# Loading the first entry's v from another queue, uncast, beside q and k

## The chip, the cores and the metric

The kernel runs on one core of a Trainium2 chip. The metric is the device time of one execution in microseconds (us); lower is better. A profile of one execution stands beside the times; its clock starts at the span's start.

## The reference

The inputs are `q`, `k`, `v` of shape (8, 8, 576, 64): 8 entries, 8 heads, 576 positions, 64 channels, fp32. Per entry and head, with `gamma = 1 - 2^(-5-head)`:

```python
scores = scale * np.matmul(q, k.transpose(0, 1, 3, 2))
Dmat = np.where(rel >= 0, gamma[:, None, None] ** rel[None, :, :], 0.0)   # rel = i - j
attn = np.matmul(scores * Dmat, v)
x = attn.transpose(0, 2, 1, 3).reshape(4608, 512)
h = x @ w_in                                   # 512 x 2048
out = (h * (1.0 / (1.0 + np.exp(-1.702 * h)))) @ w_out   # 2048 x 512
```

So it is a retention layer (linear attention with a decay, no softmax) followed by a two-layer network on 4608 tokens.

## The kernel before, in words

**Retention.** Each entry's 576 positions are cut into five pieces of 128, 128, 128, 128 and 64 rows; piece `c` of entry `b` is step `n = 5b + c`, 40 steps in all. The decay is factored: v is multiplied by `vfac` (`gamma^-pos` times the scale) when it lies on chip (`scale_v`), and the result by `gq` (`gamma^pos`) when it is evacuated (`evac_o`). A step is: `transposes(n)` (TensorE turns q and k into `psT`), `evac_t` (ScalarE copies them to `qk`), `scores` into `psS`, `mask_s` (VectorE, `psS` to `sm`), and `values`: the masked scores times v into `psO`, then k times v added to the running state in `psZ`, then the state of the earlier pieces (`zs`, which `evac_z` copies from `psZ` on ScalarE) times q. `intra(n)` is `scores` and `mask_s`; `turn(n)` is `transposes`, `evac_t`, `scale_v`. `psS`, `psT`, `psZ` are single buffers, so the next step's writer waits for this step's reader.

**Network.** The tokens go in nine chunks of 512. `hidden(c, f)` makes one of 16 column blocks of the hidden layer (four matmuls, then the activation on ScalarE); `project(c, r, g)` makes a quarter (`g`) of the sum for 128 output rows (four matmuls), and after `g = 3` VectorE copies the bank to `osb` and SP stores it. Chunk 0 needs steps 0 to 3; chunk 1 needs steps 4 to 8.

**Order.** Everything is written out by hand in one program order; a small recorder (`Rec`) gives each engine its instructions in that order and adds semaphore waits from the tiles that are read and written. An engine never overtakes its own order. First the attention steps 0 to 3, with `fill(count)`: matmuls on a zero tile into `psH[0]` that nobody reads, between the steps. Then `hidden(0, 0..15)` with step 4 between them, then `project(0, ...)`, 16 of them, with the steps 5 to 8 between them after the indices that the dictionary `between` names (`burst(n)` is `intra(n)`, `values(n-1)`, `transposes(n+1)`, `evac_t`, `finish(n-1)`, `scale_v(n+1)`, where `finish` is `evac_o` and `evac_z`). Later chunks interleave `hidden`, `project` and bursts.

**Loads.** All loads are issued by Pool (GpSimd) and cast fp32 to bf16 on the way: `load(b, c)` one piece each of q, k and v (128 rows, 128 KB as bf16), `load_w_in(i)` and `load_w_out(i)` a quarter of each weight (512 KB as bf16). Each issue keeps Pool busy while it writes the transfer's descriptors. Pool also scales v of steps 1 to 3 (`scale_v(n, "POOL")`); VectorE scales step 0 and all from step 4 on. SP issues only the stores of the result and, from step 13 on, transposing transfers. Pool's order at the start, before:

```python
load(0,0,"qk"); load(0,1,"qk"); load(0,0,"v"); load(0,2,"qk"); load(0,1,"v")
load(0,3,"qk"); load(0,2,"v"); load(0,3,"v"); load_w_in(0); scale_v(1,"POOL")
load_w_in(1); scale_v(2,"POOL"); scale_v(3,"POOL"); load(0,4)
load_w_in(2..3); load_w_out(0..3)        # then load(1, c), load(2, c)
```

Of the kernel before, what the change touches and what calls it, by code (L numbers as in the profile page):

```python
# [7 lines left out]
ALU = mybir.AluOpType  # L8
BF16 = mybir.dt.bfloat16
FP32 = mybir.dt.float32  # L10

B = 8
H = 8
S = 576
DH = 64
# [107 lines left out]
def bass_retnet_parallel__then__act_gelu_quick_kernel(  # L123
# [8 lines left out]
    P = nc.NUM_PARTITIONS  # L132
    R = Rec()
    es = ExitStack()
    with es:
        def sb(name, shape, dtype):
            return es.enter_context(nc.sbuf_tensor(name, shape, dtype))
# [14 lines left out]
        vfac = sb("vfac", [P, H, NC], FP32)  # L152
        gq = sb("gq", [P, NC, HP, 128], FP32)
        st_q = sb("st_q", [P, NST, NC, H * DH], BF16)
        st_k = sb("st_k", [P, NST, NC, H * DH], BF16)
        st_v = sb("st_v", [P, NST, NC, H * DH], BF16)
        qk = [sb(f"qk{i}", [P, 2, HP, 128], BF16) for i in range(NQK)]
        sm = [sb(f"sm{i}", [P, 2, HP, 128], BF16) for i in range(3)]
        zs = [sb(f"zs{i}", [P, HP, 128], BF16) for i in range(2)]
# [17 lines left out]
        def load(b, c, what="qkv"):  # L177
            sl, rows = b % NST, ROWS[c]
            for nm, src, dst in (("q", q, st_q), ("k", k, st_k), ("v", v, st_v)):
                if nm not in what:  # L180
                    continue
                s = src[b, :, 128 * c : 128 * c + rows, :].rearrange("h p d -> p h d")
                d = dst[0:rows, sl, c, :].rearrange("p (h d) -> p h d", d=DH)
                R.op("POOL", lambda e, d=d, s=s: e.dma_start(d, s),  # L184
                     w=[(nm, sl, c)], dma=(nm, sl, c))

        def load_w_in(i):
            s = moe_w_in.rearrange("(a p) n -> p a n", p=128)[:, :, 512 * i : 512 * i + 512]
            R.op("POOL", lambda e: e.dma_start(w_in_sb[:, :, 512 * i : 512 * i + 512], s),
                 w=[("w_in", i)], dma=("w_in", i))  # L190
# [43 lines left out]
        def constants_third(a, b):  # L234
            for t, nm in ((st_q, "q"), (st_k, "k"), (st_v, "v")):
                R.op("DVE", lambda e, t=t: e.memset(t[64:128, a:b, 4, :], 0.0),
                     w=[(nm, sl, 4) for sl in range(a, b)])

        def later_gq(hp):
            R.op("ACT", lambda e: e.activation(  # L240
                gq[:, 1:NC, hp, :], posi.ap(), AF.Exp, scale=lng[:, hp : hp + 1]),
                r=["posi", ("lng", hp, 0), ("lng", hp, 1)], w=[("gq", 1)])
# [6 lines left out]
        def scale_v(n, eng="DVE"):  # L249
            b, c = divmod(n, NC)  # L250
            sl = b % NST
            t = st_v[:, sl, c, :].rearrange("p (h d) -> p h d", d=DH)
            f = vfac[:, :, c : c + 1].to_broadcast([P, H, DH])
            R.op(eng, lambda e: e.tensor_tensor(t, t, f, ALU.mult),  # L254
                 r=["vfac"], w=[("v", sl, c)])

        def transposes(n):
            b, c = divmod(n, NC)
            sl = b % NST

            def fn(e):
                for a, t in ((0, st_q), (1, st_k)):
                    for hp in range(HP):
                        i = e.matmul(psT[:, a, hp, :], t[:, sl, c, 128 * hp : 128 * hp + 128],  # L264
                                     ident.ap(), is_transpose=True)
                return i
            R.op("PE", fn, r=["ident", ("q", sl, c), ("k", sl, c)], ps=["T"])

        def evac_t(n):
            R.op("ACT", lambda e: e.activation(qk[n % NQK].ap(), psT.ap(), AF.Copy),  # L270
                 w=[("qk", n % NQK, 0), ("qk", n % NQK, 1)], ps=["T"])
# [85 lines left out]
        def dma_turn(n):  # L357
            b, c = divmod(n, NC)
            sl, N = b % NST, ROWS[c]
            for a, t, nm, rows in ((0, st_q, "q", N), (1, st_k, "k", P)):  # L360
                R.op("SP", lambda e, a=a, t=t, rows=rows: e.dma_start_transpose(
                    out=qk[n % NQK][:, a, :, 0:rows], in_=t[0:rows, sl, c, :]),
                    r=[(nm, sl, c)], w=[("qk", n % NQK, a)], dma=("turn", n % NQK, a))

        def turn(n):
            transposes(n)
            evac_t(n)
            scale_v(n)

        def intra(n):  # L370
            scores(n)
            mask_s(n)

        def finish(n):
            evac_o(n)
            if n % NC < 4:
                evac_z(n)
            b = n // NC + NST
            if n % NC == 4 and b < B:
                for c in range(NC):  # L380
                    load(b, c)

        def burst(n):
            if n < NSTEP:
                intra(n)
            values(n - 1)
            if n + 1 < PE_TURNS:
                transposes(n + 1)
                evac_t(n + 1)
            if PE_TURNS <= n + 3 < NSTEP:  # L390
                dma_turn(n + 3)
            finish(n - 1)
            if n + 1 < NSTEP:
                scale_v(n + 1)
# [38 lines left out]

        constants_first()
        load(0, 0, "qk")
        load(0, 1, "qk")
        load(0, 0, "v")
        load(0, 2, "qk")
        load(0, 1, "v")
        load(0, 3, "qk")  # L440
        load(0, 2, "v")
        load(0, 3, "v")
        load_w_in(0)
        scale_v(1, "POOL")
        load_w_in(1)
        scale_v(2, "POOL")
        scale_v(3, "POOL")
        constants_third(0, 1)
        load(0, 4)
        for i in range(2, 4):  # L450
            load_w_in(i)
        for i in range(4):
            load_w_out(i)

        def fill(count):
            def fn(e):
                for _ in range(count):
                    i = e.matmul(psH[0].ap(), idle[:, 0:128], idle.ap(), start=True, stop=True)  # L458
                return i
            R.op("PE", fn, r=["idle"], ps=[("H", 0)])  # L460
# [13 lines left out]
        transposes(1)  # L474
        evac_t(1)
        later_gq(2)
        fill(4)
        intra(1)
        transposes(2)
        evac_t(2)  # L480
        scale_v(0)
        fill(4)
        intra(2)
        values(0, third[0])
        evac_z(0)
# [31 lines left out]
        between = {1: lambda: turn(4), 4: lambda: intra(4), 8: finish_4}  # L517
# [13 lines left out]
        def intra_9():  # L531
            intra(9)
            turn(10)

        between = {4: lambda: turn(5), 6: burst_5, 8: lambda: burst(6), 10: lambda: burst(7),
                   12: lambda: burst(8), 14: values_8}
        for i in range(16):
            r, g = divmod(i, 4)
            project(0, r, g, *wide[r % 3])
            if i in between:  # L540
                between[i]()
        between = {0: intra_9, 3: lambda: burst(10), 6: lambda: burst(11),
                   9: lambda: burst(12), 12: lambda: burst(13)}
# [93 lines left out]
```

## Time and profile before

| | |
|---|---|
| median of 3 runs | 317.63 us (317.32 to 317.97) |
| profiled execution, its own time | 317.39 us |
| its span in the trace | 315.6 us |
| TensorE busy | 304.1 us (96%), granted clock 1.00 |
| VectorE, ScalarE, Pool busy | 119.9, 130.8, 110.5 us |
| DMA engines | busy 9 tenths or more up to about 166 us |
| Pool's transfers | 116736 packets, 18.36 MB as written |

The busy share of TensorE is an average over the whole span. What it leaves idle lies in the first 41 us, at the very end, and in small pieces between. A transfer's time to landing runs from the start of its issue to the point where its semaphore shows it complete.

### The profile page before, as it was taken

The numbers are of one execution on the slowest core, as the hardware profiler recorded it, in microseconds if no ns is written. First come the engines' busy times: TensorE is split into PE (matmuls) and PEld (weight loads), VectorE is DVE, ScalarE is ACT, GpSimd is POOL, SyncE is SP. The second block draws the span as 40 slices with busy tenths as digits, with TensorE's granted clock in tenths as the row PEclk, the third lists the DMA queues.
The fourth block names the chain that finished last, engine by engine and source line by source line (L and its number), as shares of the span: only waits on it lengthen the run. The fifth ranks groups of instructions, "written<-read, shape, count | busy, mean of one in ns | idle before, by whom it ended". The sixth has DMA issues, their size and how long they took to land.

```text
span 315.6 us, 5372 instructions
## 1 busy us (share of the span) xinstructions
PE 304.1 (96%) x2272; PEld 147.8 (47%) x2315; DVE 119.9 (38%) x177; ACT 130.8 (41%) x240; POOL 110.5 (35%) x138
## 2 busy tenths in 40 slices
PE   8879999999999999999999999999999999999995
PEld 3444346445445444444444444444444444444442
DVE  5661048456335533333335333334343341010011
ACT  7676424676333333433334333333334333333300
POOL 9999688985675764333400000000000000000000
PEclk9999999999999999999999999999999999999999
DMA  9999999999999999999992233313231000001111
GB/s 73 149 173 198 195 171 168 175 170 136 151 162 175 170 173 159 174 167 126 135 122 69 64 66 81 78 40 89 72 77 50 35 34 35 33 33 55 47 65 68
DMA packets 149784, 34.83 MB, mean 110 GB/s; under 512 B 141056, under 2 KB 145152, under 8 KB 149760
## 3 DMA queue, kind: packets, MB, share of 16 engines
q0 software_dynamic: 116736, 18.36, 84.5%
q1 hardware_dynamic: 33024, 16.13, 23.6%
q8 instruction: 18, 0.29, 0.4%
q14 instruction: 6, 0.05, 0.0%
HBM read 36.70 MB, written 9.44 MB: 146 GB/s over the span
## 4 chain that ended last, share of the span: by engine, by line
PE 85%; DMA 7%; POOL 5%; issue 1%; DVE 0%; ACT 0%; POOLq 0%
PE psH L406 35%; PE psU L420 33%; DMA w_out_sb<-in_moe_w_out_dram 5%; PE psH L420 4%; PE psO L303 4%; PE psS L282 3%; PE psO L327 3%; DMA st_v<-in_v_dram 2%; POOL st_k L184 1%; PE psT L264 1%; POOL st_q L184 1%; PE psZ L316 1%; PE psO L420 1%; POOL st_v L184 1%; POOL w_out_sb L194 1%
## 5 line engine op out<-in xcount | busy, mean ns | idle before, releaser
L411 ACT ACTIVATE gT<-psH 128x512 bf16<-128x512 f32 x144 | 85.8, 597 | 135.9 <-PE psH L406 135.9
L406 PE MATMUL psH<-xT,w_in_sb 128*128 128x512 bf16 x559 | 137.7, 379 | 2.4 <-DVE xT L353 0.8
L420 PE MATMUL psU<-w_out_sb,gT 128*128 128x512 bf16 x475 | 118.7, 379 | 2.1 <-DMA w_out_sb<-in_moe_w_out_dram 1.0
L406 PEld LDWEIGHTS psH<-xT,w_in_sb 128*128 128x128 bf16 x576 | 54.2, 98 | 66.7 <-ACT gT L411 5.1
L291 DVE TENSOR_TENSOR sm<-psS,mask 128x1024 bf16<-128x1024 f32 (+1 forms) x40 | 44.7, 1117 | 105.5 <-PE psS L282 105.5
L420 PEld LDWEIGHTS psU<-w_out_sb,gT 128*128 128x128 bf16 x496 | 47.5, 98 | 55.1 <-issue 1.4
L428 DVE COPY osb<-psU 128x512 f32<-128x512 f32 x31 | 21.4, 691 | 65.6 <-PE psU L420 64.9
L184 POOL DMA_DIRECT2D st_k<-in_k_dram x40 | 34.7, 866 | 29.6 <-PE psO L327 15.7
L184 POOL DMA_DIRECT2D st_v<-in_v_dram x40 | 34.6, 868 | 12.0 <-PE psO L327 5.9
L184 POOL DMA_DIRECT2D st_q<-in_q_dram x40 | 35.1, 878 | 7.5 <-issue 7.0
L344 ACT ACTIVATE zs<-psZ 64x256 bf16<-64x256 f32 x64 | 24.1, 377 | 13.8 <-PE psZ L316 12.9
L353 DVE TENSOR_TENSOR xT<-psO,gq 128x512 bf16<-128x512 f32 (+1 forms) x38 | 23.8, 627 | 9.4 <-PE psO L327 8.8
L254 DVE TENSOR_TENSOR st_v<-st_v,vfac 128x512 bf16<-128x512 bf16 x37 | 25.2, 682 | 2.4 <-DMA st_v<-in_v_dram 2.4
L270 ACT ACTIVATE qk<-psT 128x1024 bf16<-128x1024 bf16 x13 | 13.3, 1023 | 17.6 <-PE psT L264 17.5
L282 PEld LDWEIGHTS psS<-qk 64*128 64x128 bf16 x320 | 8.6, 94 | 18.0 <-issue 15.7
L282 PE MATMUL psS<-qk 64*128 64x128 bf16 (+1 forms) x320 | 15.0, 213 | 0.9 <-ACT qk L270 0.9
L303 PE MATMUL psO<-sm,st_v 128*64 128x128 bf16 (+1 forms) x304 | 14.9, 220 | 0.0
L420 PE MATMUL psH<-w_out_sb,gT 128*128 128x512 bf16 x62 | 14.5, 379 | 0.1
L458 PE MATMUL psH<-idle 128*128 128x512 bf16 x33 | 10.9, 468 | 1.3 <-DVE idle L206 1.2
L303 PEld LDWEIGHTS psO<-sm,st_v 128*64 128x64 bf16 x304 | 9.2, 109 | 4.9 <-issue 1.7
L327 PE MATMUL psO<-qk,zs 128*128 128x128 bf16 (+1 forms) x120 | 11.0, 215 | 0.0
L316 PE MATMUL psZ<-st_v,st_k 128*64 128x64 bf16 x256 | 9.3, 195 | 0.0
(48 smaller groups left out, 78.7 us busy)
## 6 DMA issues: line engine op xcount, KB each, us to landing
out_dram<-osb SPq DMA_DIRECT2D x36, 256.0 KB, 2.3
st_q<-in_q_dram POOLq DMA_DIRECT2D x32, 128.0 KB, 17.9
st_k<-in_k_dram POOLq DMA_DIRECT2D x32, 128.0 KB, 17.9
st_v<-in_v_dram POOLq DMA_DIRECT2D x32, 128.0 KB, 18.3
w_in_sb<-in_moe_w_in_dram POOLq DMA_DIRECT2D x4, 512.0 KB, 7.9
w_out_sb<-in_moe_w_out_dram POOLq DMA_DIRECT2D x4, 512.0 KB, 14.2
st_q<-in_q_dram POOLq DMA_DIRECT2D x8, 64.0 KB, 18.5
st_k<-in_k_dram POOLq DMA_DIRECT2D x8, 64.0 KB, 18.8
```

The costliest lines, as they stand in the source:

```text
L184: R.op("POOL", lambda e, d=d, s=s: e.dma_start(d, s), w=[(nm, sl, c)], dma=(nm, sl, c))
L254: R.op(eng, lambda e: e.tensor_tensor(t, t, f, ALU.mult), r=["vfac"], w=[("v", sl, c)])
L282: i = e.matmul(psS[:, hh, hp, 0:N], t[rows, 1, hp, :], t[rows, 0, hp, 0:N])
L291: R.op("DVE", lambda e: e.tensor_tensor(o, i, m, ALU.mult), r=["mask"], w=[("sm", n % 3)], ps=["S"])
L303: i = e.matmul(po[64 * hh : 64 * hh + 64, hp, 0:N], st_v[:, sl, c, 64 * h : 64 * h + 64], sm[n % 3][:, hh, hp, 0:N], start=(hp == 0), stop ...
L327: i = e.matmul(po[:, hp, 0:N], zs[(c - 1) % 2][:, hp, :], qk[n % NQK][:, 0, hp, 0:N], start=False, stop=True, skip_group_check=True)
L344: R.op("ACT", lambda e, rows=rows: e.activation(zs[c % 2][rows, :, rows], psZ[rows, :, 0:64], AF.Copy), w=[("zs", c % 2, hh)], ps=["Z"])
L353: R.op("DVE", lambda e: e.tensor_tensor(xT[:, :, t0 : t0 + N], po[:, :, 0:N], gq[:, c, :, 0:N], ALU.mult), r=[("gq", min(c, 1))], w=[("xT" ...
L406: i = e.matmul(psH[t].ap(), w_in_sb[:, a, 128 * f : 128 * f + 128], xT[:, a, 512 * c : 512 * c + 512], start=(a == 0), stop=(a == 3))
L411: R.op("ACT", lambda e: e.activation(gT[c % 2][:, f, :], psH[t].ap(), AF.Gelu_apprx_sigmoid), w=[("gT", c % 2, f)], ps=[("H", t)])
L420: i = e.matmul(bank, gT[c % 2][:, f, 128 * r : 128 * r + 128], w_out_sb[:, f, :], start=(f == 0), stop=(f == NF - 1))
L428: R.op("DVE", lambda e: e.tensor_copy(osb[m].ap(), bank), w=[("osb", m)], ps=[key])
```

## The change

- v of entry 0, pieces 0 to 3, is no longer loaded by Pool as bf16. SP loads it as fp32 into a new tile `v32`.
- SP is held back by a tile `flag`: Pool sets one column of it (a `memset`) at the place in its order at which it has written the q and k pieces ahead of it; SP's transfer waits for that column. Piece 0 follows q and k of piece 1, piece 1 follows those of piece 2, pieces 2 and 3 follow those of piece 3.
- `scale_v` for these four reads `v32` and writes bf16 into `st_v`.
- In Pool's order piece 4 of entry 0 now goes ahead of `w_in` 1, and `w_in` 1, 2 and 3 stand between the three scalings.
- On VectorE `scale_v(0)` moves ahead of `mask_s(1)`; the fills before `intra(1)` and `intra(2)` go from 4 and 4 matmuls to 3 and 2.
- Among the projections of chunk 0 the bursts stand one index later, but for the last, `values_8`, which stays after 14.

```diff
+        v32 = sb("v32", [P, 4, H * DH], FP32)
+        flag = sb("flag", [P, 4], FP32)
...
+        def load_v32(c):
+            R.op("POOL", lambda e: e.memset(flag[:, c : c + 1], 0.0), w=[("flag", c)])
+            s = v[0, :, 128 * c : 128 * c + 128, :].rearrange("h p d -> p h d")
+            d = v32[:, c, :].rearrange("p (h d) -> p h d", d=DH)
+            R.op("SP", lambda e: e.dma_start(d, s), r=[("flag", c)], w=[("v32", c)], dma=("v32", c))
...
-            R.op(eng, lambda e: e.tensor_tensor(t, t, f, ALU.mult),
-                 r=["vfac"], w=[("v", sl, c)])
+            first = b == 0 and c < 4
+            i = v32[:, c, :].rearrange("p (h d) -> p h d", d=DH) if first else t
+            R.op(eng, lambda e: e.tensor_tensor(t, i, f, ALU.mult),
+                 r=["vfac"] + ([("v32", c)] if first else []), w=[("v", sl, c)])
...
-        load(0, 0, "v")
+        load_v32(0)
         load(0, 2, "qk")
-        load(0, 1, "v")
+        load_v32(1)
         load(0, 3, "qk")
-        load(0, 2, "v")
-        load(0, 3, "v")
+        load_v32(2)
+        load_v32(3)
         load_w_in(0)
+        constants_third(0, 1)
+        load(0, 4)
         scale_v(1, "POOL")
         load_w_in(1)
         scale_v(2, "POOL")
+        load_w_in(2)
         scale_v(3, "POOL")
-        constants_third(0, 1)
-        load(0, 4)
-        for i in range(2, 4):
-            load_w_in(i)
+        load_w_in(3)
...
-        fill(4)
+        fill(3)
+        scale_v(0)
         intra(1)
         transposes(2)
         evac_t(2)
-        scale_v(0)
-        fill(4)
+        fill(2)
         intra(2)
...
-        between = {4: lambda: turn(5), 6: burst_5, 8: lambda: burst(6), 10: lambda: burst(7),
-                   12: lambda: burst(8), 14: values_8}
+        between = {5: lambda: turn(5), 7: burst_5, 9: lambda: burst(6), 11: lambda: burst(7),
+                   13: lambda: burst(8), 14: values_8}
```

## The prediction

> **What bounds the kernel now.** TensorE is busy 96% of the span, so I looked first for the places where it stands idle, in its timeline up to 60 us and in the waits after that. Behind 45 us the only wait of TensorE over 0.2 us is one of 0.65 us at 70.3, for ScalarE. The change touches nothing there, so the time moves by what happens before. These are the stops that matter (start, busy, instruction, count, idle before it and what ended it):
>
> ```profile
> 11.31 0.38 PE L264 MATMUL psT<-ident,st_q 128*128 128x128 bf16 x4 [0.39 <-DMA st_k<-in_k_dram]
> 13.12 0.40 PE L282 MATMUL psS<-qk 64*128 64x128 bf16 x8 [0.34 <-ACT qk L270]
> 14.09 0.38 PE L264 MATMUL psT<-ident,st_q 128*128 128x128 bf16 x4
> ...
> 20.36 1.67 PE L406 MATMUL psH<-xT,w_in_sb 128*128 128x512 bf16 x7 [0.77 <-DVE xT L353]
> 22.89 0.38 PE L264 MATMUL psT<-ident,st_q 128*128 128x128 bf16 x4 [0.86 <-DMA st_k<-in_k_dram]
> ...
> 36.27 2.75 PE L420 MATMUL psU<-w_out_sb,gT 128*128 128x512 bf16 x11
> 40.01 1.02 PE L420 MATMUL psU<-w_out_sb,gT 128*128 128x512 bf16 x4 [0.98 <-DMA w_out_sb<-in_moe_w_out_dram]
> ```
>
> The first network matmul starts at 20.36; `transposes(4)` waits 0.86 us for k; three projections end at 39.02 and the fourth, at 40.01, waits for the last quarter of `w_out`. The chain that ended last says the same (start, us, what):
>
> ```profile
> 19.12 1.53 POOL w_in_sb L189 x2
> 20.65 2.14 POOL w_out_sb L194 x3
> 22.79 17.08 DMA w_out_sb<-in_moe_w_out_dram
> 40.01 1.02 PE psU L420 x4
> ```
>
> Issued at 22.79, that quarter lands at 39.87: the queue of transfers sets 40.01, and behind it TensorE runs without a stop. So there are two clocks: the transfers' (40.01) and TensorE's own (without the stop at `transposes(4)`, 40.01 - 0.98 - 0.86 = 38.17). The later one counts. Next I read what the DMA engines moved, in slices of 0.5 us, from 2 to 22 and from 40 to 60 us:
>
> ```profile
> GB/s 0 0 56 134 91 81 131 144 149 128 139 135 135 145 137 149 150 144 148 152 150 151 156 145 136 149 180 175 182 207 176 141 182 203 205 188 182 166 130 113
> GB/s 154 156 153 156 153 154 155 155 155 154 154 217 274 241 154 154 155 153 152 152 183 143 204 252 203 161 159 155 155 155 167 152 155 155 158 322 273 158 155 186
> ```
>
> In the second row Pool's q, k and v pieces alone give a flat 155 GB/s as written: that is the engines' limit for these small packets, 131 KB / 155 = 0.85 us a piece. Weights run at 203 to 209 GB/s (rows from 24 to 36 us). The first row stays below both: Pool issues a piece every 0.87 us, and around 17.5 and 20.5 to 22 us the rate drops while Pool scales v and issues step 4's half pieces late.
>
> **The change, part by part.**
>
> *Pool's issues.* Four v issues go, 4 x 0.87 = 3.5 us; four memsets come, at most 0.10 us each (the constants' memsets at 0.24 us). q and k of piece 2 start 0.76 us sooner (5.15 instead of 5.91), of piece 3 1.5 us (6.99), `w_in` 0 at 8.9 instead of 11.97.
>
> *What that is worth to the transfers.* The engines have to move the same pieces; they gain only where they were starved. From 7 to 14 us they ran at 145 on average: (155 - 145)/155 x 7 = 0.43 us. From 14 to 23 us they moved 1511 KB: 98 KB of pieces left over (0.63 us), 197 KB of step 4 (1.27) and 1216 KB of weights at 206 (5.9), 7.8 us of work in 9: 1.2 us. Together 1.6 us. Will Pool keep ahead there now? The scaling of piece 1 waits for `v32`; SP's transfer starts at 6.99 and, if it takes the 5.6 to 6.7 us of SP's four stores between 41 and 60 us, lands at 12.6 to 13.7. Then come a scaling (1.1 us, two took 2.25) and `w_in` 1, written by 14.6 to 15.7, while the engines have `w_in` 0 and step 4 to do until about 18. Scalings 2 and 3 end by 16.8 and 18.7; piece 3's v was used at 18.60, so there 0.1 us may show.
>
> *A v piece as fp32.* The same 1024 packets, the same 256 bytes read, twice the bytes written. No row shows it. Cheapest: the weights' rate, 412 GB/s read, 0.64 us a piece, 4 x 0.21 = 0.8 us less. Dearest: 155 GB/s written holds for it too, 1.69 us, 3.4 us more in all. I take 0.85, no difference, since these packets are nearest in count and read size to the cast pieces; so 1.6 us stands, between 2.4 sooner and 1.8 later.
>
> *VectorE's order.* `scale_v(0)` (0.68 us) now waits for `v32` ahead of `mask_s(1)`; behind that are `psS` and with it `intra(2)`, `values(0)`, `transposes(3)`, all in TensorE's order. Released at about 5.15 and with SP's 5.6 to 6.7 us, v lands at 10.8 to 11.9; plus 0.68 and 1.14 (mask) and 0.1, `intra(2)` can start at 12.7 to 13.8; before it started at 13.12, after ScalarE's `qk`. From 13.12 to the last `values` TensorE had no stop, so TensorE's clock moves by this: 0.4 sooner (bounded by `transposes(2)`, whose 0.39 us wait can go) to 0.7 later; I take 0.1 later. The three fills taken out (0.216 us each) stood beside ScalarE's 1.02 us copy of `qk`, with 0.34 us idle behind them: nothing gained.
>
> *Step 4 ahead of `w_in` 1.* k lands some 3 us sooner; the 0.86 us stop goes. `w_in` 1 is then about 22 at the latest, needed at 24.5. So TensorE's clock is at 38.17 + 0.1 = 38.3, the transfers' at 40.01 - 1.6 = 38.4. Gain about 1.5 us after rounding for the two meeting.
>
> *The projections.* Between `burst(8)` and `values_8` there are now four matmuls instead of eight. The state of step 8 needs `psZ`, which ScalarE empties after the copy of `transposes(9)`:
>
> ```profile
> 54.98 1.02 ACT L270 ACTIVATE qk<-psT 128x1024 bf16<-128x1024 bf16 x1 [1.63 <-PE psT L264]
> 55.90 0.75 ACT L344 ACTIVATE zs<-psZ 64x256 bf16<-64x256 f32 x2
> ...
> 56.84 0.29 PE L316 MATMUL psZ<-st_v,st_k 128*64 128x64 bf16 x8
> ```
>
> `psZ` is free at 56.65 and the state ran at 57.01 by the chain, 0.36 us later. One projection less (0.86 us) turns that into a stop of about 0.56 us with the semaphore's 0.06; it delays all of chunk 1. What the move covers: `transposes(5)` at 41.86 came just behind k's landing at 41.8, and so did those of steps 6 and 7; with transfers and TensorE both sooner they'd stay level, so that cover is worth 0 here (up to 0.5 if TensorE gets ahead).
>
> *Sum.* -1.5 + 0.56 = -0.94 us. On the profiled execution's 317.39 (1.8 us of it outside the span, unchanged) that is 316.45; the median lies 0.24 above that execution, so 316.7.
>
> **Rivals.**
>
> *SP's transfers bring extra throughput.* If packets of a second queue went beside Pool's, the transfers' clock would move by up to 1.6 + 3.4 us and TensorE's would count: 38.17 - 0.4 = 37.8, gain 2.25, with the stop 1.7: 315.9. Against it: at 45.5 to 47 us a store of 262 KB passes, 366 KB move in all, and of 232 KB of pieces only 104 go through; the store takes 0.83 us of the engines. For it: the fp32 pieces need no cast, a price no row shows.
>
> *Freed Pool time is worth nothing.* The engines' total stays what it was, since the fp32 pieces take up the 1.6 us (0.4 us each above the cast ones); then 40.01 holds and the stop is added: 318.2, and with 1.69 us a piece 320. The Trainium skill (DMA: Bandwidth & Descriptors, "Issuing engines are not separate DMA queues") has it that transfers of any issuer run on the same 16 engines, so that several issuers save only the time to issue. The displaced pieces at 45.5 us agree; by that rule alone the gain would be 0 and the time 318.2.
>
> *v0 comes late and holds VectorE: slower.* The slowest of SP's transfers took 8.6 us to land (a transposing one). Released at 5.15, v0 would land at 13.75, `mask_s(1)` end at 15.6, `intra(2)` start at 15.67, 2.55 us later than now; TensorE's clock becomes 38.17 + 2.55 = 40.7, with the stop +1.26: 318.9. It turns slower when TensorE's clock is past 39.45, that is when v0 lands later than 12.45 us. For it: under Pool's load SP's stores took 5.6 to 6.7 us instead of 2.0. Against it: when v0 starts, Pool's backlog is only about three pieces.
>
> *No effect.* If Pool's memsets ran ahead of the descriptors, v would contend earlier; Pool has been in order in the timeline, so little chance.
>
> **How the numbers follow.** A run can tell about 0.2%, 0.63 us, from nothing. Forecast 0.47, of which 0.09 within 0.63 us (the starved time is smaller than worked out); extra throughput 0.15; freed time worth nothing 0.15, 0.07 of it within 0.63 us, 0.08 beyond; late v0 0.19; no effect 0.04. Faster 0.38 + 0.15 = 0.53; same 0.09 + 0.07 + 0.04 = 0.20; slower 0.08 + 0.19 = 0.27. The range goes from a little below the extra-throughput case (315.6) to the late v0 (318.9); the forecast's own is 315.9 to 317.3.
>
> **What would show it.** `w_out`'s last quarter landing near 38.3; no stop at `transposes(4)`; `v32` landing by 12 us, with `mask_s(1)` not after 12.7; a stop of about 0.6 us on `psZ` before the state of step 8; a DMA rate near 155 from 7 to 14 us (well above, counted with v's doubled bytes, means throughput was added). A fourth projection at 40 or later, or `mask_s(1)` beginning after 13, would prove me wrong.

## The result and the profile after

The changed kernel takes 320.08 us (median of 5 runs, 319.38 to 320.74) against 317.93 for the kernel before beside it: ratio 1.0071, 95% interval 1.0049 to 1.0093. It is slower by 2.2 us, and outside the range that was forecast. The profiled execution took 320.04 us with a span of 318.2, 2.6 more than before.

TensorE's timeline of the changed kernel, the rows that answer to those shown of before (start, busy, instruction, count, idle before it and what ended it):

```profile
9.89 0.38 PE L274 MATMUL psT<-ident,st_q 128*128 128x128 bf16 x4 [1.05 <-DMA st_k<-in_k_dram]
12.82 0.38 PE L274 MATMUL psT<-ident,st_q 128*128 128x128 bf16 x4 [0.71 <-DMA st_k<-in_k_dram]
14.63 0.61 PE L292 MATMUL psS<-qk 64*128 64x128 bf16 x8 [0.77 <-ACT qk L280]
16.32 0.59 PE L274 MATMUL psT<-ident,st_q 128*128 128x128 bf16 x4 [0.29 <-DMA st_k<-in_k_dram]
24.68 1.67 PE L416 MATMUL psH<-xT,w_in_sb 128*128 128x512 bf16 x7 [0.77 <-DVE xT L363]
26.20 0.39 PE L274 MATMUL psT<-ident,st_q 128*128 128x128 bf16 x4
39.62 3.62 PE L430 MATMUL psU<-w_out_sb,gT 128*128 128x512 bf16 x15
59.46 0.32 PE L326 MATMUL psZ<-st_v,st_k 128*64 128x64 bf16 x8 [0.56 <-ACT zs L354]
```

The transposes of steps 1, 2 and 3 come 1.2, 1.5 and 2.2 us later than before (8.70, 11.31, 14.09), each behind a wait for k. The first network matmul is 4.32 us late (24.68 instead of 20.36). The stops at step 4 (26.20) and at the last quarter of `w_out` (all four projections run on from 39.62) are gone, and the one on `psZ` is there. In sums from start to start: +4.32 at the first network matmul; from there to the first projection 14.94 instead of 15.91 us, -0.97; from there to `transposes(5)` (44.80, one projection of 0.86 us more) 4.32 instead of 5.62, -1.30; +0.56 on `psZ`: 2.6 us in all.

How late k was, in the chain that ended last, up to step 3's transposes (start, us, what):

```profile
7.70 8.48 DMA st_k<-in_k_dram
16.18 0.14 issue
16.32 1.01 PE psT L274 x8
```

Pool issued this piece at 7.70 instead of 9.37, and it took 8.5 instead of 4.6 us to land: issued 1.7 us sooner, landed 2.2 us later. k of pieces 1 and 2 took 5.6 and 6.7 us (before 4.3 and 4.4). SP's four v pieces took 5.1, 6.3, 9.2 and 11.8 us. The last two were issued at about 8.8 and 9.2 us, just behind `w_in` 0 (8.64). Pool's scalings of pieces 1, 2 and 3 each stood still for their v, in its own timeline:

```profile
13.40 1.06 POOL L264 TENSOR_TENSOR st_v<-v,vfac 128x512 bf16<-128x512 f32 x1 [1.88 <-DMA v<-in_v_dram]
18.07 1.05 POOL L264 TENSOR_TENSOR st_v<-v,vfac 128x512 bf16<-128x512 f32 x1 [2.84 <-DMA v<-in_v_dram]
21.02 1.05 POOL L264 TENSOR_TENSOR st_v<-v,vfac 128x512 bf16<-128x512 f32 x1 [1.14 <-DMA v<-in_v_dram]
```

And something that no rival had. The busy times by stage, again of the changed kernel (start and end, length, then the busy time of TensorE, of its weight loads, of VectorE, ScalarE and Pool; behind them the granted TensorE clock, the DMA share, which passes 1 where packets overlap on an engine, and GB/s):

```profile
8.00:10.00 2.00, 0.70 (x11) 0.36 (x11) 1.11 (x1) 1.00 (x2) 2.00 (x5) 1.00 1.92 172
10.00:12.00 2.00, 1.44 (x19) 0.79 (x17) 0.80 (x2) 1.46 (x2) 1.52 (x3) 1.00 1.89 205
12.00:14.00 2.00, 1.09 (x13) 0.57 (x10) 1.23 (x1) 0.70 (x2) 0.60 (x1) 1.00 1.89 176
```

TensorE, kept waiting, was busy for 0.70 of the 2 us from 8 to 10 (before 1.75), 1.44 from 10 to 12 (before 1.22) and 1.09 from 12 to 14 (before 1.65): 3.23 us of six instead of 4.62. Then the granted clock fell to 0.50, from 14.28 to 21.10 us:

```profile
10.86:14.28 3.42, 1.68 (x19) 0.83 (x18) 1.38 (x2) 2.12 (x3) 1.54 (x2) 1.00 1.85 186
14.28:17.69 3.41, 2.77 (x34) 2.08 (x34) 1.82 (x2) 1.29 (x4) 0.95 (x2) 0.50 1.31 188
17.69:21.10 3.41, 3.19 (x32) 1.75 (x32) 0.16 (x1) 2.06 (x4) 1.89 (x3) 0.50 1.60 173
```

Before, it was 1.00 from 8 to 22 us.

### The profile page after: what moved, and what is told of

It reads as the page before. It is cut to its first block, busy times and chain, and to the rows that moved or that the text cites. A ratio compares the mean times of both kernels' runs of the same rounds, so it can differ in the third digit from the quotient of the medians.

```text
span 318.2 us, 5371 instructions
## 1 busy us (share of the span) xinstructions
PE 304.7 (96%) x2270; PEld 148.7 (47%) x2312; DVE 119.9 (38%) x177; ACT 130.8 (41%) x240; POOL 107.2 (34%) x138
## 4 chain that ended last, share of the span: by engine, by line
PE 92%; DMA 3%; POOL 2%; issue 1%; ACT 1%; DVE 0%; POOLq 0%
PE psH L416 39%; PE psU L430 33%; PE psH L430 4%; PE psO L313 4%; PE psS L292 4%; PE psO L337 3%; DMA st_k<-in_k_dram 3%; PE psT L274 2%; PE psZ L326 1%; POOL st_q L186 1%; PE psO L430 1%; PE psH L468 1%; POOL st_k L186 1%; ACT qk L280 0%; DVE xT L363 0%
## 5 line engine op out<-in xcount | busy, mean ns | idle before, releaser
L186 POOL DMA_DIRECT2D st_v<-in_v_dram x36 | 31.0, 861 | 16.6 <-issue 8.5
L264 DVE TENSOR_TENSOR st_v<-st_v,vfac 128x512 bf16<-128x512 bf16 x36 | 24.5, 682 | 0.0
L292 PEld LDWEIGHTS psS<-qk 64*128 64x128 bf16 x320 | 8.9, 96 | 19.1 <-issue 18.4
L468 PE MATMUL psH<-idle 128*128 128x512 bf16 x30 | 10.0, 464 | 1.5 <-DVE idle L214 1.2
## 6 DMA issues: line engine op xcount, KB each, us to landing
st_q<-in_q_dram POOLq DMA_DIRECT2D x32, 128.0 KB, 16.8
```

Of the source, the lines that this page charges most:

```text
L186: R.op("POOL", lambda e, d=d, s=s: e.dma_start(d, s), w=[(nm, sl, c)], dma=(nm, sl, c))
L264: R.op(eng, lambda e: e.tensor_tensor(t, i, f, ALU.mult), r=["vfac"] + ([("v32", c)] if first else []), w=[("v", sl, c)])
L292: i = e.matmul(psS[:, hh, hp, 0:N], t[rows, 1, hp, :], t[rows, 0, hp, 0:N])
```

## The experiments

Three theories stood at the start. **A:** SP's pieces, in a queue of their own, take the engines' time ahead of k; TensorE waits and its clock falls. **B:** the fp32 pieces, with twice the written bytes, are dear in whichever queue. **C:** the moved weights, fills and projections cost the time.

**The whole change without SP.** `load_v32(c)` becomes `load(0, c, "v")` at the same four places; all the rest stays as changed.

> The changed kernel with v of the first entry loaded by Pool and cast again, at the places of the flags; the order of the weights, the fills and the projections stay as changed. Theory A (SP's second queue takes the engines' time ahead of k, TensorE idles and its clock falls): transposes of steps 1, 2, 3 at 8.7, 11.3, 14.1 us as in the kernel before, granted clock 1.00 throughout, first network matmul at 20.4 to 21.6 us (the scaling of piece 3 now ends near 19.7), in all 317.6 to 318.2 us. Theory C (the moved weights, fills and projections cost the time, not SP): 319.5 to 320.5 us, and the clock falls here too.

Measured: 317.11 us, ratio to before 0.9995 (0.9982 to 1.0008), clock 1.00.

```profile
11.44 0.38 PE L272 MATMUL psT<-ident,st_q 128*128 128x128 bf16 x4 [0.22 <-DMA st_k<-in_k_dram]
14.30 0.38 PE L272 MATMUL psT<-ident,st_q 128*128 128x128 bf16 x4 [0.18 <-DMA st_k<-in_k_dram]
16.02 0.41 PE L311 MATMUL psU<-sm,st_v 128*64 128x128 bf16 x8 [0.68 <-POOL st_v L262]
```

Steps 2 and 3 are back within 0.2 us of their old times, so theory C falls: the rest of the change is worth about nothing in sum. It isn't free inside: step 4's pieces ahead of the scalings made values(1) wait 0.68 us for Pool, and the first network matmul is at 21.45.

**The same pieces as fp32, but in Pool's queue.** `load_v32` issues on Pool, uncast, without the flag.

> The changed kernel with the fp32 v loaded uncast by Pool, in one queue with q and k, no flags. Theory A: one queue keeps the order, so k of pieces 1, 2, 3 come as with the cast v (transposes at 8.7, 11.3, 14.1 us) and the time is that of the cast one within 0.4 us. Theory B (the fp32 pieces with their doubled written bytes are dear, whichever queue): with 1.7 instead of 0.85 us a piece, steps 2 and 3 come 0.8 and 1.7 us later than with the cast v, v of piece 3 some 3.4 us later, and the time is 1 to 2 us above it.

Measured: 317.66 us, ratio 0.9997 (0.9983 to 1.0012).

```profile
12.04 0.38 PE L273 MATMUL psT<-ident,st_q 128*128 128x128 bf16 x4 [0.78 <-DMA st_k<-in_k_dram]
15.04 0.38 PE L273 MATMUL psT<-ident,st_q 128*128 128x128 bf16 x4 [0.32 <-DMA st_k<-in_k_dram]
```

0.60 and 0.74 us later than with the cast v, with one and two fp32 pieces ahead; v of piece 3 lands at 17.2 instead of 16.1, with four. That is 0.27 us a piece over the four (0.60 for the first alone), less than theory B's 0.85, and the time is the same within its interval. B gives a small part, not the loss.

**SP's loads alone.** The kernel before, with only `load_v32` in place of the four v loads.

> The kernel before with nothing changed but v of the first entry by SP as fp32 with the flags; order of weights, scalings, fills and projections as before. Theory A: k of pieces 1 to 3 late as in the changed kernel (transposes near 9.9, 12.8, 16.3 us), v of pieces 2 and 3 late behind w_in 0, and step 4's pieces, now issued after all scalings, land near 27 us, so at least the changed kernel's time without its 0.56 us: 319.5 to 321.5 us. Theory C: 317.6 us, no change.

Measured: 325.10 us, ratio 1.0248 (1.0223 to 1.0274), slower than the 319.5 to 321.5 that were expected. Steps 2 and 3 turn at 12.65 and 16.73, as A has it; the scaling of piece 3 waited 3.89 us for `v32`, started at 23.37, and everything that stands behind the scalings in Pool's order (step 4, three quarters of `w_in`, `w_out`) came late with it: `w_out` stopped TensorE ahead of 45.04 and again, for 1.65 us, ahead of 47.51. In the changed kernel, which has the weights between the scalings, `w_out` stopped TensorE nowhere.

**k first.** In the changed kernel all four flags stand behind k of piece 3.

> The changed kernel with all four v pieces released only when Pool has written k of piece 3. Theory A (SP's pieces take the engines' time ahead of k): k of pieces 1, 2, 3 lands near 8.5, 10.4 to 11.0 and 12.4 to 13.0 us, 1 to 3 us sooner than in the changed kernel; the v pieces, all behind and beside w_in 0, land from 14 to 22 us, VectorE and step 0's values wait for them, and the whole is slower still, 320 to 322 us. If Pool's issues or the engines' own start were what made k late: k lands at 9.8, 12.7 and 16.2 us again.

Measured: 322.92 us in two runs, 0.9 above the range, ratio 1.0149 (1.0105 to 1.0194). k of pieces 1, 2, 3 landed at 8.8, 10.6 and 12.8 us, 0.9, 2.1 and 3.4 us sooner than in the changed kernel, though Pool issued it at the same times to 0.1 us: SP's pieces had been in its way. How they were shows in the packets of the two queues. From 8 to 9 us the kernel before moved 1110 packets, all Pool's. In the changed kernel (packets, MB, share; first 8 to 9 us beside q and k, then 16 to 18 us beside the weights and step 4's pieces):

```profile
q0 software_dynamic: 500, 0.06, 98.2%
q1 hardware_dynamic: 497, 0.13, 72.5%
q0 software_dynamic: 501, 0.24, 87.7%
q1 hardware_dynamic: 496, 0.12, 47.2%
```

q0 is Pool's queue, q1 SP's. While both had work, they got the same number of packets: SP's queue took half of the turns, and k's queue went on at half its pace.

In the run with k first VectorE waits instead, and with it TensorE (VectorE's row, then TensorE's):

```profile
16.40 0.69 DVE L264 TENSOR_TENSOR st_v<-v,vfac 128x512 bf16<-128x512 f32 x1 [6.28 <-DMA v<-in_v_dram]
18.29 0.61 PE L292 MATMUL psS<-qk 64*128 64x128 bf16 x8 [6.13 <-DVE sm L301]
```

**Only two pieces by SP.** Pieces 2 and 3 of v by Pool, cast, behind k of piece 3.

> The changed kernel with only v of pieces 0 and 1 by SP; pieces 2 and 3 by Pool, cast, behind k of piece 3. Theory A: k of pieces 1 and 2 as late as in the changed kernel (transposes near 9.9 and 12.8 us), k of piece 3 sooner, near 14.5 us, since two of SP's four pieces are gone; v of pieces 2 and 3 land by 17 us in Pool's own queue, ahead of w_in 0 instead of beside it; the clock falls less or not at all; 317.5 to 318.5 us, most of the loss gone. If the loss lay in the first two pieces: 319.5 us or more.

Measured: 317.23 us, ratio 0.9987 (0.9968 to 1.0006), clock 1.00.

```profile
12.86 0.38 PE L274 MATMUL psT<-ident,st_q 128*128 128x128 bf16 x4 [0.59 <-DMA st_k<-in_k_dram]
15.93 0.38 PE L274 MATMUL psT<-ident,st_q 128*128 128x128 bf16 x4 [0.39 <-DMA st_k<-in_k_dram]
22.20 1.67 PE L416 MATMUL psH<-xT,w_in_sb 128*128 128x512 bf16 x7 [0.77 <-DVE xT L363]
```

k is nearly as late as in the changed kernel (step 3 at 15.93, where 14.5 was expected), and still the loss is gone: the first network matmul is 1.84 us later than before (1.23 in the profile of the run with the same order and the old projections, below), and the two stops that go, 0.86 and 0.98, pay for that. So the late k costs about what the change brings, and the loss itself comes with pieces 2 and 3 by SP.

**What delays pieces 2 and 3.** In the changed kernel `w_in` 0 and step 4 go behind the scaling of piece 1.

> The changed kernel with w_in 0 and step 4's pieces behind the scaling of piece 1 in Pool's order, so that nothing of Pool's but the rest of q and k moves beside SP's v. If the weights' packets beside them make v of pieces 2 and 3 late: these land near 14.5 and 16 us instead of 17.9 and 20.9, the scaling of piece 3 is done by 20 us, and the first network matmul comes at 22 to 23 us; w_in 0, written at 15.2, lands near 22.5 and step 4's k near 23.5, where they may stop TensorE for up to 1 us; 318 to 319.5 us. If SP's queue is slow by itself with four such pieces: 17.9 and 20.9 us again, and 320.5 us or more.

Measured: 318.49 us, ratio 1.0046 (1.0026 to 1.0067). The two pieces land near 16.2 and 17.5 us instead of 18.0 and 20.9, and the scalings wait no more for them:

```profile
18.46 1.12 POOL L264 TENSOR_TENSOR st_v<-v,vfac 128x512 bf16<-128x512 f32 x1
20.30 1.07 POOL L264 TENSOR_TENSOR st_v<-v,vfac 128x512 bf16<-128x512 f32 x1
```

So the transfers of the weights and of step 4 beside them made piece 3 3.4 us late, which is not all of its lateness: the two were expected at 14.5 and 16. The clock fell in the profiled execution too (0.50 from 14.42 to 21.25 us), and the first network matmul came at 24.91, not at 22 to 23. The nine runs fall in two groups by the clock: five with a mean clock of 0.998 or more took 318.01 to 318.49 us, four with 0.988 to 0.995 took 319.51 to 320.56.

**Fills against the clock.** The changed kernel with 15 more fills (the expectation counts 16) where TensorE had waited.

> The changed kernel with 16 more fills, each put where TensorE stood idle in its profile (2 ahead of step 0, 4 and 2 around step 1, 3 and 3 around step 2, 1 ahead of step 3), none long enough to delay what follows. If the halved clock between 14 and 21 us costs the time: the clock stays at 1.00, the first network matmul comes at 22.6 instead of 24.68 us and the time falls by about 2 us to 318. If the late v sets it (the scaling of piece 3's v ended at 22.07 us, and the matmuls from there to the first network matmul took 1.8 us): the clock stays up, the first network matmul comes at 23.8 to 24.0 us and the time falls by 0.7 us to 319.3.

Measured: 321.07 us, ratio 1.0084 (1.0054 to 1.0114). Half of it came as expected: the clock stayed at 1.00 up to 22 us, and the first network matmul came at 23.82, as the late v would have it. Then it fell one stage later, on the network's first matmuls:

```profile
22.29 0.41 PE L313 MATMUL psH<-sm,st_v 128*64 128x128 bf16 x8 [1.27 <-POOL st_v L264]
23.82 3.53 PE L416 MATMUL psH<-xT,w_in_sb 128*128 128x512 bf16 x8 [0.54 <-DVE xT L363]
```

Eight matmuls in 3.53 us are 0.44 each instead of 0.216; from 20 to 22 us TensorE had been busy for 0.97 of 2 us, waiting for piece 3. The fills moved the loss of clock, and no time was won. One of the six runs had a mean clock of 0.998 and took 318.88 us; the other five, at 0.993 to 0.995, took 321.02 to 321.86.

**The projections.** The changed kernel with the old `between`.

> The changed kernel with the projections' bursts back at the old indices. All theories: the stop of 0.56 us on psZ before the state of step 8 goes, and transposes(5) finds its k long there (the transfers are ahead of TensorE by some 3 us), so 0.5 to 0.6 us less than the changed kernel, about 319.5 us. If the later indices covered a late k, a wait for st_k shows instead and the time does not fall.

Measured: 319.58 us, ratio 1.0069 (1.0046 to 1.0092). The stop on `psZ` is gone from the profile, and no wait for k took its place; but the start of this profiled execution was 1.2 us later than the changed kernel's (first network matmul at 25.85), and the runs spread by 2.2 us. The 0.5 us can't be read from these times; the next two runs bear on it. Nor do these six runs go by the clock: 318.96 us at a mean of 0.989, 319.41 at 0.998.

**Versions that might beat both.** Five pieces of the change were left standing: step 4 ahead of `w_in` 1, weights between the scalings, `scale_v(0)` ahead of `mask_s(1)`, fewer fills, and SP for the first two pieces. First, two pieces by SP and the old projections:

> The kernel with only v of pieces 0 and 1 by SP, now with the projections' bursts at the old indices. In its profile TensorE waited for nothing between 22 and 56 us and then 0.56 us on psZ. If that stop is all that the later indices cost, it goes: 0.5 to 0.6 us less, 316.6 to 316.8 us, 0.2 to 0.4% below the kernel before. If the later indices cover a late k of steps 5 to 7, a wait for st_k of 0.3 to 0.6 us shows at their transposes and the time stays at 317.2.

Measured: 316.81 us, ratio 0.9980 (0.9965 to 0.9995). Between the first network matmul at 21.59 and 69 us TensorE waited for nothing. Then no piece by SP and the old projections:

> The changed kernel with v by Pool, cast, and the projections' bursts at the old indices: nothing by SP, the new order of weights and the fewer fills remain. The stop on psZ goes and TensorE's clock and the last quarter of w_out (39.3 us) meet as before: 316.5 to 316.8 us. The same rival: a wait for st_k at steps 5 to 7, 317.1 us.

Measured: 316.73 us, ratio 0.9976 (0.9962 to 0.9991), the lowest of all. k of steps 6 and 9 comes just in time:

```profile
44.00 0.38 PE L272 MATMUL psT<-ident,st_q 128*128 128x128 bf16 x4 [0.15 <-DMA st_k<-in_k_dram]
53.99 0.38 PE L272 MATMUL psT<-ident,st_q 128*128 128x128 bf16 x4 [0.15 <-DMA st_k<-in_k_dram]
```

Both are faster than before by 0.6 to 0.9 us, and between the two no difference is shown.

**Other orders of Pool.** The kernel before with step 4 behind the scaling of piece 1 and piece 3 scaled by VectorE:

> The kernel before with v by Pool, cast, and of the change only this: step 4's pieces go ahead of w_in 1 (behind the scaling of piece 1), and piece 3's v is scaled by VectorE behind evac_o of step 0. Fills and projections as before. All theories: the wait of 0.86 us at transposes(4) goes, Pool's scalings are in time for values(1) and values(2), and the last quarter of w_out, the later clock, lands at 39.0 to 39.4 instead of 39.87 us; 0.5 to 0.9 us less than before, 316.6 to 317.0 us.

Measured: 317.08 us, ratio 0.9982 (0.9963 to 1.0002): 0.7 us less than before beside it, within what was expected, but not settled. The last quarter of `w_out` let the fourth projection start at 39.49 instead of 40.01. And with both scalings ahead of `w_in` 1:

> The kernel before with step 4's pieces ahead of w_in 1, behind the scaling of piece 1, and with the scalings of pieces 2 and 3 ahead of w_in 1 on Pool. The wait at transposes(4) goes (0.86 us); the scaling of piece 3 ends near 18.3 us, in time for values(3) at 18.6; w_in 1 is written by 19.1 us, which can leave the engines idle around 20 us for up to 0.6 us, so the last quarter of w_out lands at 39.2 to 39.9: 316.9 to 317.6 us.

Measured: 317.72 us, 0.1 above the range, ratio 0.9997 (0.9982 to 1.0012). What the engines moved from 2 to 22 us, in slices of 0.5 us:

```profile
GB/s 0 0 41 125 111 65 129 130 152 150 142 149 128 152 132 135 132 156 154 154 154 138 147 153 160 180 188 176 207 187 184 150 134 61 34 21 46 110 206 207
```

From 18.5 to 20.5 us they moved little (21 to 61 GB/s), longer than expected; the gain was probably spent there. (Its profiled execution, 319.44 us, was the slowest of its 13 runs; only this row of it is used.)

## Why the prediction was wrong

**The step that failed** is TensorE's clock: "0.4 sooner ... to 0.7 later; I take 0.1 later". It let `intra(2)` hang on VectorE and v0 alone, and took k's landing to follow Pool's issues, which indeed came sooner. Measured: 4.32 us later at the first network matmul. Two more runs split it, one profiled execution each: 1.84 with two pieces by SP (22.20: k late); 1.62 more with four and the clock kept up (23.82: pieces 2 and 3 late, in TensorE's order and in Pool's); 0.86 more with the clock halved (24.68). Profiles of kernels that are alike up to there differ by 0.61 (22.20 and 21.59) and 1.17 us (24.68 and 25.85), so each term is good to about 1 us only. That k and pieces 2 and 3 are late, and that the loss goes when Pool loads pieces 2 and 3 (ratio 0.9987 against 1.0071), doesn't hang on the split. The prediction's own rows had the reason at hand: the engines were at their limit of 155 GB/s and a store by SP pushed aside 128 KB of pieces. I used that row against the rival of extra throughput, and did not go on to ask what v pushes aside.

The Trainium skill (DMA: Bandwidth & Descriptors, "Queues, rings and completion order") says that each engine goes round the queues it has work for, a packet at a time. Theory A is what that makes of this change: a second queue is a second turn, for v ahead of k that was issued before it. The trace agrees: 500 of Pool's packets and 497 of SP's from 8 to 9 us, and k landed 0.9 to 3.4 us sooner with SP's queue empty. It also agrees that a turn is not a share of bytes: from 16 to 18 us 501 packets of Pool's carried 0.24 MB, 496 of SP's 0.12, and SP's piece 3 landed 3.4 us sooner without that traffic.

**The transfers' gain**, 1.6 us, was too large. The last quarter of `w_out`, issued at 25.0 instead of 22.79, took 16.0 us and landed at 41.0: 1.1 us later than before, not 1.6 sooner. The runs split this too: with Pool's new order and cast v it landed near 39.2 (22.5 and 16.7), 0.7 sooner; with fp32 v in Pool's queue near 39.9, 0.7 dearer (the step took "no difference"); with SP at 41.0, 1.1 more. Pool, which was to be ahead, was late: scalings 2 and 3 ended at 19.1 and 22.1, where 16.8 and 18.7 were worked out, because SP's transfers were priced at 5.6 to 6.7 us by stores with 2 KB packets and took up to 11.8. TensorE came for that quarter at 42.3 only, so none of this shows in the time.

**What held.** v0 landed by 10.3 us, a little sooner than worked out, VectorE waited only 0.21 us for it, and `mask_s(1)` began at 12.14, ahead of the 13 that was named as a sign of being wrong (the other sign, a fourth projection at 40 or later, came: 42.3); the stop at `transposes(4)` went; the new stop on `psZ` was 0.56 us, to the hundredth. Taking it out moved the ratios of like kernels from 0.9987 to 0.9980 and from 0.9995 to 0.9976, 0.2 and 0.6 us, the right way though each within the intervals. The cover of the later indices was put at 0 to 0.5; two waits of 0.15 us were all that showed.

**The rivals.** None came true as told. "v0 late" was on the right side, at 318.9, and only by luck: its mechanism was another; VectorE was hardly held, k was late. "Freed Pool time is worth nothing" was true of the transfers and too mild: they came later still, and it left TensorE's clock where it was. The sign named for extra throughput came true in bytes and not in packets: 185 GB/s from 8 to 13 us, well above 155, but 5552 packets where the kernel before moved 5799. So that sign misleads here: SP's packets carry twice the bytes, and the engines passed no more of them.

**The clock.** The Trainium skill (TensorE: Matmul & The Clock Gate, Part 1) ties the halved clock to a window of about 3.4 us that runs freely, and puts the fall behind an idle window. The length agrees. In seven of the fourteen profiles the clock fell before 300 us; each time it stayed at 0.50 for 3.41 or 6.83 us, and had been at 1.00 for 10.24, 17.07, 20.48 or 34.13 us, whole multiples of 3.41 (read by narrowing the stretches of the view until the clock changes). The idle window does not agree: here the longest idle row between the clock's rise at 4.04 us and its fall was 1.05 us, and TensorE was busy for 1.68 of the last 3.41 us (the row from 10.86).

Cut the time at full clock into stretches of 3.41 us, counted from the clock's rise, and the two cases separate in all fourteen profiles up to 300 us: in the stretch just ahead of each of the seven falls TensorE was busy for 0.99 to 1.76 us, and in no other stretch for less than 1.92. With two pieces by SP the least was 2.21. So in these traces the fall goes with a load below about half of a stretch, not with one long gap. The bound is not sharp: one stretch behind 310 us, at the kernel's end, had 1.61 us and no fall behind it. The rise came anywhere from 4.04 to 7.05 us, so the same waits can lie in one stretch or be split between two; that this is why the runs of one kernel differ was not tested.

What the fall costs is less sure. The changed kernel's one run at a mean clock of 1.00 took 319.38 us, its four below that 320.04 to 320.74; the run with `w_in` 0 behind has 1.7 us between the means of its groups, the one with more fills at least 2.1. The six runs with the old `between` don't go by the clock at all. And a late transfer can both lengthen a run and lower its clock, so these differences are no clean price.

## What to carry to other kernels

When the DMA engines are at their limit, moving a load to another queue doesn't make room; it moves that load ahead of others, so list what waits in the old queue and price each as late by what the new one takes, a packet for a packet. Where a queue of small packets must run beside one of large packets, expect it last, and don't put an in-order engine's next work behind it. An issue that comes sooner is no landing that comes sooner: check the rate first.

## What was not expected of the hardware

- SP's 256 KB pieces took 5.1 us to land beside q and k, and up to 11.8 us (13.8 in the run with SP's loads alone) beside a weight quarter, which itself took 10.6 instead of 7.4.
- The granted clock fell to 0.50, for 3.41 or 6.83 us, behind stretches of 3.41 us in which TensorE had been busy for 0.99 to 1.76 us.
- Two queues with work got the same number of packets: 500 and 497 beside q and k, 501 and 496 beside the weights and step 4's pieces, where Pool's carried twice the bytes of SP's.
- VectorE's scaling of a v piece took 1.94 us instead of 0.68 where Pool scaled another beside it (15.92 and 16.21, in the run with piece 3 on VectorE), from its start until after Pool's end at 17.31. It is one instance; at 12.57 in the same run VectorE kept its 0.68 and Pool's scaling, begun at 12.82, took 1.34 instead of 1.10.
